# Sliding-window attention and two feed-forward layers on one core: weights rescaled seven block products behind their loads, x loaded a phase ahead

## The chip, the cores and the metric

One NeuronCore of a Trainium2 chip runs the whole program. The metric is the device time of one execution in microseconds; the median of several runs is compared. All times below are microseconds unless they say ns.

## The reference

```python
# attention: B=4, H=8, S=576, D=64, window 128, a slope per head
scores = scale * np.matmul(q, k.transpose(0, 1, 3, 2))
scores = np.where(mask, scores + bias[None], -1000000000.0)   # 0 <= i - j < 128
attn = softmax(scores)                                        # rows
x = np.matmul(attn, v) -> (2304 tokens, 512)
# layer 1: ELU                     # layer 2: SiLU
h = x @ w_in       # 512 -> 2048   h = x @ w_in
g = where(h > 0, h, exp(min(h,0)) - 1)   g = h * (1 / (1 + exp(-h)))
x = g @ w_out      # 2048 -> 512   out = g @ w_out
```

The weights arrive as 64-bit floats, q, k, v as 32-bit floats. The answer is wanted at 32-bit accuracy.

## The kernel before, in words

**Arithmetic.** Every 32-bit operand of a matmul is cut into an upper part (`...h`, a rounded copy made by ScalarE) and a lower part (`...l`, the difference, made by VectorE or GpSimd); a product is three matmuls, h·h, h·l and l·h. The products with `w_in` use a Strassen-like scheme: for a pair of two weight blocks and a block of 768 tokens, seven block products (`m1`, `m2`, `m6`, `m5`, `m7`, `m4`, `m3`, six matmuls each) take the place of eight.

**Phases.** `attention()` runs first and fills TensorE's idle time with the first four of 16 blocks of layer 1 (`hidden`, `output`). Then `layers()` runs: what is left of that filling (called the opening here), and then 15 steps `k`, written `(layer, sweep, token block)`. A sweep is a range of the 16 weight blocks (`SWEEPS`), and the three token blocks of 768 pass one after another. Step 0 to 2 and 3 to 5 are sweeps 1 and 2 of layer 1, steps 6 to 8, 9 to 11 and 12 to 14 are the sweeps of layer 2. A step is `nq` quads of seven block products, and then `outputs(k)`: 24 pieces (layer 1) or 18 (layer 2) of six matmuls each. The first quad of the next step takes the last two pieces along (`pend`), and each quad's `m4` and `m3` are made in the next quad or among the output pieces (`left_over`).

**Order.** The order on every engine is that in which the Python code issues instructions (`manual_schedule`), and every engine works through its own list in order: an instruction that waits holds all behind it on that engine. After each block product and each output piece `between(where)` is called. It moves each chain of activations one stage on (`chain`: `bent` exp or sigmoid on ScalarE, `act` on VectorE, `upper` the `gh` on ScalarE, `lower` the `gl` on GpSimd or VectorE), takes tasks from `xtasks`, and makes one step of the weights.

**Weights.** 128 x 512 blocks of 64-bit numbers are loaded into four raw tiles (`wraw`, `NRAW`), in the order of `tasks`. Each passes through four stages: `rescale` (GpSimd on the high words, line 144, and ScalarE on the low words, line 146), `sign` and `join` (VectorE, lines 151 and 156), and `part`, which makes the upper and lower parts. For `w_in` the second block of a pair first gets four sums on GpSimd (lines 186 to 189), and then `wbh`, `wch`, `wdh` on ScalarE with their lower parts on VectorE. Only then are the pair's two raw tiles free, and the loads that were issued into them on SyncE's queue can start. `weight_step(loaded, which, lag)` may take each stage once in a call; `rescale` follows its load by at least `lag` calls, and `part` waits for room in `made`/`room`. `room` for a new pair opens when the last step of a sweep has used the old one, so the weights of the next sweep are made during steps 2, 5, 8 and 11.

**x.** `make(k)` gives the tasks that make the seven operands of a new token block (`NAMES`, single buffered). Its two halves `c` are the even and the odd 128-row chunks of x. For layer 1 `begin(c)` loads the half from DRAM into `xs` (one buffer); for layer 2 it is taken from the accumulator. GpSimd makes four sums (lines 689 to 692), ScalarE the upper and VectorE the lower parts. Token blocks that come again are kept in DRAM (`keep`) and read back (`reload`).

```python
                calls[0] += 1
                weight_step(0, ((4, 1), (2, 3))[calls[0] % 2], 1)      # after an output piece
            elif where == "h":                                        # after a block product:
                calls[0] += 1                                         # every second time
                turn[0] += 1
                if turn[0] % 2 == 0:
                    weight_step(0, ((4, 1), (2, 3))[turn[0] // 2 % 2], 1)
```

Of the kernel before, what the change touches and what calls it, by code (L numbers as in the profile page):

```python
# [17 lines left out]
P = 128  # L18
# [24 lines left out]
def attention_elu_silu_kernel(  # L43
# [41 lines left out]
    OUTS = 7  # L85
    OPEN = 5
    ORDER = ((0, 1, 2), (2, 1, 0)), ((2, 1, 0), (0, 1, 2), (2, 1, 0))
    WSLOTS = [*range(15), *range(26, 34)]
# [556 lines left out]
    def layers(fill):  # L645
        pair_p.append(left("pair", PAIRS))
        c_p = left("combo", 1)
        h_p = left("hh", 2)
        e_p = left("ee", 3)
        t_p = left("tt", 1)  # L650
# [13 lines left out]
        NAMES = "b11", "b21", "b22", "t4", "t1", "t2", "t3"  # L664
        FIRST_USE = 0, 1, 5, 4, 6, 3, 2

# [5 lines left out]
        def make(k):  # L672

            layer, sw, b = steps[k]
            out = []
            src = {}

            def begin(c):
                if layer == 0:
                    src[c] = t = t_p.tile([P, 2, BIG], F32, tag="xs", name="xs")  # L680
                    nc.sync.dma_start(t, x_dram[b][:, c::2, :])
                else:
                    src[c] = acc[b].rearrange("p (c t) -> p c t", c=NKC)[:, c::2, :]

            def sums(c):
                b11, b12, b21, b22 = (src[c][:, i, j * HALF:(j + 1) * HALF] for i in range(2) for j in range(2))
                t2, t3, t4 = (t_p.tile([P, HALF], F32, tag=t, name=t) for t in ("t2", "t3", "t4"))
# [19 lines left out]
            def all_sums(c):  # L707
                for fn in sums(c):
                    fn()
            order = FIRST_USE  # L710
# [47 lines left out]
        def quad(k, q, last):  # L758
# [56 lines left out]
            def m4():  # L815
                product(3, "b", False)
                activated(t["b"][:, 0:HALF], 1, 0)
                if b == steps_last(k):
                    room[0] += 2

            def m3():
                product(2, "c", False)
                add("s2", "c")
                activated(t["s2"], 0, 1)
            return m1, m2, m6, m5, m7, m4, m3

# [55 lines left out]

        turn = [0]

        def between(where):
            chain()
            if where == "y":
                for _ in range(2):
                    if xtasks:
                        xtasks.pop(0)()  # L890
                calls[0] += 1
                weight_step(0, ((4, 1), (2, 3))[calls[0] % 2], 1)
            elif where == "h":
                calls[0] += 1
                turn[0] += 1
                if turn[0] % 2 == 0:
                    weight_step(0, ((4, 1), (2, 3))[turn[0] // 2 % 2], 1)

        for fn in make(0):
            xtasks.append(fn)  # L900
        seq = list(fill)
# [22 lines left out]
        while xtasks:  # L924
            xtasks.pop(0)()
        early.close()
# [5 lines left out]
        for k, (layer, sw, b) in enumerate(steps):  # L932
            nq = (SWEEPS[layer][sw][1] - SWEEPS[layer][sw][0]) // 2
            left_over = None
            for q in range(nq):
                for key in ((0, layer, SWEEPS[layer][sw][0] + 2 * q + 1),):
# [24 lines left out]
            while xtasks:  # L961
                xtasks.pop(0)()
        while chains:
# [36 lines left out]
```

## Time and profile before

| | |
|---|---|
| median of 3 runs | 1083.8 (1083.4 to 1087.84) |
| the profiled execution | 1088.96, of it span 1086.8 |
| TensorE matmul busy | 913.9 of the span (84%), mean granted clock 0.911 |
| VectorE busy | 631.8 (58%) |
| ScalarE busy | 490.6 (45%) |
| GpSimd busy | 423.6 (39%) |

How to read it: attention ends near 200, the opening near 252, and the 15 steps fill the rest. The granted clock is a share of full speed; in the trace it stands at one of two levels, 2.4 GHz and 1.2 GHz, and 128 x 384 matmuls of layer 1 begin 0.17 apart at the one level and 0.32 at the other. An engine's idle time counts only where TensorE ends up waiting for it.

### The profile page before, as it was taken

What the parts mean: (1) busy time and instruction counts of PE and PEld (TensorE: products, weight loads), DVE (VectorE), ACT (ScalarE), POOL (GpSimd) and SP (SyncE); (2) the same over time, 40 slices, a digit from 0 to 9 for tenths busy, and PEclk for the clock granted to TensorE, in tenths of its full rate; (3) what the DMA queues carried; (4) which work ended last, traced back from release to release, by engine and by line L of the source; (5) the groups of instructions that cost most, each with busy time, mean ns of one, the idle gap of its engine ahead of it and who ended that gap; (6) DMA issues with size and microseconds to landing.
All of it is one profiled execution on the core that took longest, in us unless ns stands there. A gap on an engine that the chain in (4) does not pass through costs nothing.

```text
span 1086.8 us, 15260 instructions
## 1 busy us (share of the span) xinstructions
PE 913.9 (84%) x5520; PEld 807.0 (74%) x5520; DVE 631.8 (58%) x1241; ACT 490.6 (45%) x1155; POOL 423.6 (39%) x514
## 2 busy tenths in 40 slices
PE   6789999954577997497999629989988899979998
PEld 4566767733577996397999629879876789968987
DVE  7866567345566766646464665767464643555444
ACT  6676667333542535334142444555544423344322
POOL 8643333146354435626141653625253411241111
PEclk9889999976778998798999869989988999989999
DMA  8324442211734211217050125251322605022551
GB/s 286 98 85 126 145 143 93 69 39 68 280 106 173 89 30 40 78 39 262 19 204 1 39 77 232 88 203 48 157 78 77 243 40 204 1 77 92 209 224 58
DMA packets 54923, 125.50 MB, mean 115 GB/s; under 512 B 3648, under 2 KB 35648, under 8 KB 54848
## 3 DMA queue, kind: packets, MB, share of 16 engines
q1 hardware_dynamic: 54704, 124.40, 32.0%
q8 instruction: 43, 0.70, 0.3%
q14 instruction: 32, 0.26, 0.1%
q10 hardware_dynamic: 144, 0.13, 0.0%
HBM read 87.56 MB, written 36.96 MB: 115 GB/s over the span
## 4 chain that ended last, share of the span: by engine, by line
PE 50%; DVE 14%; POOL 12%; issue 8%; ACT 8%; DMA 8%; SPq 0%; POOLq 0%; ACTq 0%; DVEq 0%
PE y L862 22%; PE b L775 10%; PE c L775 4%; DMA wraw<-in_moe_w_out_dram 4%; PE a L525 3%; POOL gl L755 3%; PE h L272 3%; DVE e L255 2%; PE a L775 2%; DMA wraw<-in_moe_w_in_dram 2%; DVE e L256 2%; PE y L308 2%; DVE wraw L151 2%; PE s L447 2%; PE pt L486 2%
## 5 line engine op out<-in xcount | busy, mean ns | idle before, releaser
L755 POOL TENSOR_TENSOR gl<-e,gh 128x384 fp32r<-128x384 f32 x120 | 128.9, 1079 | 303.7 <-ACT gh L751 242.9
L862 PE MATMUL y<-gh,w1h 128*128 128x384 f32 x288 | 102.8, 357 | 38.0 <-ACT gh L751 38.0
L751 ACT ACTIVATE gh<-e 128x384 fp32r<-128x384 f32 x168 | 86.4, 522 | 98.8 <-DVE e L256 60.7
L862 PE MATMUL y<-w1h,gl 128*128 128x512 f32 (+1 forms) x292 | 116.2, 398 | 5.4 <-DVE gl L755 5.4
L862 PE MATMUL y<-w1h,gh 128*128 128x512 f32 (+1 forms) x292 | 116.0, 397 | 5.0 <-ACT gh L751 5.0
L862 PE MATMUL y<-w1l,gh 128*128 128x512 f32 (+1 forms) x292 | 115.4, 395 | 0.0
L862 PE MATMUL y<-gl,w1h 128*128 128x384 f32 x288 | 103.6, 360 | 13.0 <-POOL gl L755 13.0
L151 DVE SCALAR_TENSOR_TENSOR wraw<-wraw 128x512 uint32<-128x512 uint32 x60 | 64.7, 1079 | 80.6 <-POOL wraw L144 80.6
L862 PE MATMUL y<-gh,w1l 128*128 128x384 f32 x288 | 101.5, 353 | 0.0
L506 POOL TENSOR_SCALAR p<-p,sm 128x192 f32<-128x192 f32 (+1 forms) x144 | 61.3, 444 | 101.4 <-DVE sm L464 91.4
L875 DVE TENSOR_TENSOR acc<-y,acc 128x384 f32<-128x384 f32 (+2 forms) x85 | 50.3, 605 | 74.4 <-PE y L862 74.4
L255 DVE TENSOR_SCALAR e<-e 128x384 f32<-128x384 f32 (+2 forms) x92 | 53.4, 580 | 64.3 <-ACT e L748 34.8
L862 PEld LDWEIGHTS y<-gh,w1h 128*128 128x128 f32 x288 | 58.1, 202 | 40.9 <-ACT gh L751 40.9
L146 ACT ACTIVATE wraw<-wraw 128x512 int32<-128x512 uint32 x60 | 40.2, 670 | 98.4 <-DMA wraw<-in_moe_w_out_dram 61.0
L460 ACT ACTIVATE p<-p,neg 128x192 f32<-128x192 f32 (+1 forms) x144 | 62.9, 439 | 31.7 <-DVE neg L455 31.7
L144 POOL TENSOR_SCALAR wraw<-wraw 128x512 f32<-128x512 f32 x60 | 41.3, 688 | 91.6 <-DMA wraw<-in_moe_w_out_dram 59.2
L166 POOL TENSOR_TENSOR w1l<-wraw,w1h 128x512 fp32r<-128x512 f32 x28 | 39.4, 1405 | 85.8 <-ACT w1h L165 85.8
L862 PEld LDWEIGHTS y<-w1h,gl 128*128 128x128 f32 x292 | 56.5, 193 | 19.4 <-DVE gl L755 7.1
L862 PEld LDWEIGHTS y<-gl,w1h 128*128 128x128 f32 x288 | 58.1, 202 | 16.8 <-POOL gl L755 16.7
L775 PE MATMUL b<-t,wdh 128*128 128x384 f32 x168 | 46.8, 361 | 25.9 <-ACT h L782 25.9
L862 PEld LDWEIGHTS y<-w1h,gh 128*128 128x128 f32 x292 | 56.8, 194 | 15.7 <-ACT gh L751 5.9
L782 ACT ACTIVATE hs<-b 128x384 f32<-128x384 f32 x42 | 20.4, 487 | 104.4 <-PE b L775 104.4
(146 smaller groups left out, 2391.0 us busy)
## 6 DMA issues: line engine op xcount, KB each, us to landing
t<-d SPq DMA_DIRECT2D x24, 768.0 KB, 6.7
wraw<-in_moe_w_in_dram SPq DMA_DIRECT2D x32, 512.0 KB, 4.1
d<-t SPq DMA_DIRECT2D x20, 768.0 KB, 6.2
wraw<-in_moe_w_out_dram SPq DMA_DIRECT2D x28, 512.0 KB, 3.6
b<-d SPq DMA_DIRECT2D x18, 768.0 KB, 5.6
d<-b SPq DMA_DIRECT2D x15, 768.0 KB, 4.5
k<-in_k_dram SPq DMA_DIRECT2D x16, 384.0 KB, 5.0
v<-in_v_dram SPq DMA_DIRECT2D x18, 256.0 KB, 2.8
```

The source lines that it names most:

```text
L144: nc.gpsimd.tensor_scalar(f32(top), f32(top), 2.0 ** -112, 1.0, op0=ALU.mult, op1=ALU.mult)
L146: nc.scalar.activation(low.bitcast(I32), low, AF.Copy, scale=7.49 * 2.0 ** -32)
L151: nc.vector.scalar_tensor_tensor(low, top, 0x80000000, low, op0=ALU.bitwise_and, op1=ALU.bitwise_or)
L166: eng.tensor_tensor(lo[:, o:o + w], f32(src), f32(h[:, o:o + w]), op=ALU.subtract)
L255: nc.vector.tensor_scalar(e, e, 1.0, -1.0, op0=ALU.min, op1=ALU.add)
L460: nc.scalar.activation(dst, dst, AF.Exp, bias=m, scale=-1.0, accum_out=a)
L506: nc.gpsimd.tensor_scalar(dst, dst, by, 1.0, op0=ALU.mult, op1=ALU.mult)
L751: nc.scalar.activation(gh[:, s], tiles["e"], AF.Copy)
L755: eng.tensor_tensor(gl[:, s], tiles["e"], f32(gh[:, s]), op=ALU.subtract)
L775: nc.tensor.matmul(t[name][:, 0:HALF], a[:, cs], x[:, j, c, :], start=(start and c == 0 and n == 0), stop=(c == 1 and n == 2), skip_group_ ...
L862: nc.tensor.matmul(t["ps"][:, 0:w], l, r, start=(f == 0 and x == 0), stop=(f == n - 1 and x == 2))
L875: nc.vector.tensor_tensor(dst, t["ps"][:, 0:w], dst, op=ALU.add)
```

## The change

**The lag.** Every `between` now makes one step of the weights, after block products too, and `rescale` follows its load by seven calls (`LAG`) and not by one. **x.** `make(k + 1)` is called at the start of step `k`, and `begin(0)` with it, so the load of the first half is issued some 21 block products before its sums; in layer 1 the sums then stand behind 21 empty tasks, and the second half's load and sums have 21 more between them. Three tasks are taken per output piece (`POPS`) and not two. The operands are made in the order b21, b11, t2, t1, t3, t4, b22, about the order in which the products of the step before let go of their places; the fourth sum is made later and in the place of `b21`, not in a tile of its own. **e.** The pool of activation tiles has four buffers and not three. **Room** for a new pair opens after `m3` and not after `m4`.

```diff
@@ class constants
+    LAG = 7
+    POPS = 3
@@ layers
-        e_p = left("ee", 3)
+        e_p = left("ee", 4)
@@ make
             def sums(c):
                 b11, b12, b21, b22 = (...)
-                t2, t3, t4 = (...)
-                src[c] = b11, b21, b22, t4, b12, t2, t3
-                return [lambda: nc.gpsimd.tensor_tensor(t3, b22, b12, op=ALU.subtract),
-                        lambda: nc.gpsimd.tensor_tensor(b12, b12, b11, op=ALU.subtract),
-                        lambda: nc.gpsimd.tensor_tensor(t2, b22, b12, op=ALU.subtract),
-                        lambda: nc.gpsimd.tensor_tensor(t4, b21, t2, op=ALU.subtract)]
+                t2, t3 = (...)
+                src[c] = b11, b21, b22, b21, b12, t2, t3
+                nc.gpsimd.tensor_tensor(t3, b22, b12, op=ALU.subtract)
+                nc.gpsimd.tensor_tensor(b12, b12, b11, op=ALU.subtract)
+                nc.gpsimd.tensor_tensor(t2, b22, b12, op=ALU.subtract)
+
+            def last_sum(c):
+                nc.gpsimd.tensor_tensor(src[c][1], src[c][1], src[c][5], op=ALU.subtract)
...
-            for c in range(2):
-                out.append(lambda c=c: (begin(c), all_sums(c)))
-                for x, i in enumerate((0, 1, 2, 6, 4, 5, 3)):
-                    out.append(lambda c=c, i=i: upper(c, i))
-                    if x:
-                        out.append(lambda c=c, i=last: lower(c, i))
-                    last = i
-                out.append(lambda c=c, i=last: lower(c, i))
+            def spread(c):
+                out = [lambda: sums(c)]
+                order = 1, 0, 5, 4, 6, 3, 2
+                for x, i in enumerate(order):
+                    out.append(lambda i=i: upper(c, i))
+                    if x:
+                        out.append(lambda i=order[x - 1]: lower(c, i))
+                    if x == 2:
+                        out.append(lambda: last_sum(c))
+                out.append(lambda: lower(c, order[-1]))
+                return out
+            begin_first = lambda: begin(0)
+            wait = [None] * (POPS * LAG if layer == 0 else 0)
+            out = spread(0) + [lambda: begin(1)] + wait + spread(1)
             if again(k):
                 out += [lambda i=i: keep(i) for i in range(7)]
-            return out
+            return begin_first, wait + out
@@ m4, m3: "room[0] += 2" moves from m4 to m3
@@ between
             if where == "y":
-                for _ in range(2):
+                for _ in range(POPS):
                     if xtasks:
-                        xtasks.pop(0)()
-                calls[0] += 1
-                weight_step(0, ((4, 1), (2, 3))[calls[0] % 2], 1)
-            elif where == "h":
-                calls[0] += 1
-                turn[0] += 1
-                if turn[0] % 2 == 0:
-                    weight_step(0, ((4, 1), (2, 3))[turn[0] // 2 % 2], 1)
+                        fn = xtasks.pop(0)
+                        fn and fn()
+            calls[0] += 1
+            weight_step(0, ((4, 1), (2, 3))[calls[0] % 2], LAG)
@@ the steps
+            if k + 1 < len(steps) and source(k + 1) == "make":
+                begin, ahead = make(k + 1)
+                begin()
             for q in range(nq):
...
             if k + 1 < len(steps) and source(k + 1) == "make":
-                xtasks.extend(make(k + 1))
+                xtasks.extend(ahead)
```

TensorE's own order is the same in both. **ScalarE in step 2**, around the first pair of the next sweep, before (`hs<-b` is the snap of a quad's first product, `wbh`, `wch`, `wdh` the upper parts of the pair, `wraw<-wraw` the rescaling of a block that has just been loaded, `h_...<-b` the snap of `m6`, for which `m7` waits):

```order
L782 ACTIVATE hs<-b 128x384
L751 ACTIVATE gh<-e 128x384
L748 ACTIVATE e<-hs 128x384
L165 ACTIVATE wbh<-wraw 128x256
L165 ACTIVATE wch<-wraw 128x512
L165 ACTIVATE wdh<-wraw 128x512
L146 ACTIVATE wraw<-wraw 128x512
L748 ACTIVATE e<-b 128x384
L782 ACTIVATE h_4386<-b 128x384
```

The same place in the changed kernel:

```order
L786 ACTIVATE hs<-b 128x384
L167 ACTIVATE wbh<-wraw 128x256
L167 ACTIVATE wch<-wraw 128x512
L167 ACTIVATE wdh<-wraw 128x512
L755 ACTIVATE gh<-e 128x384
L752 ACTIVATE e<-hs 128x384
L752 ACTIVATE e<-b 128x384
L786 ACTIVATE h_4378<-b 128x384
```

The rescaling has left the place ahead of the snap (it now stands behind the next pair's `wdh`), and the pair's upper parts stand one product earlier.

**GpSimd at the start of the opening**, before (`t<-xs` and `xs<-xs` are the sums of x for step 0, `wal` and `gl` lower parts, lines 186 to 189 a pair's sums, line 144 the rescaling):

```order
L689 TENSOR_TENSOR t_2893<-xs 128x384
L690 TENSOR_TENSOR xs<-xs 128x384
L691 TENSOR_TENSOR t_2892<-xs 128x384
L692 TENSOR_TENSOR t_2894<-xs,t_2892 128x384
L166 TENSOR_TENSOR wal<-wraw,wah 128x512
L291 TENSOR_TENSOR gl<-e,gh 128x512 x2
L186 TENSOR_TENSOR wraw<-wraw 128x256
L187 TENSOR_TENSOR wraw<-wraw 128x256
L188 TENSOR_TENSOR wraw<-wraw 128x256
L189 TENSOR_TENSOR wraw<-wraw 128x256
L144 TENSOR_SCALAR wraw<-wraw 128x512
```

and in the changed kernel:

```order
L168 TENSOR_TENSOR wal<-wraw,wah 128x512
L293 TENSOR_TENSOR gl<-e,gh 128x512 x2
L188 TENSOR_TENSOR wraw<-wraw 128x256
L189 TENSOR_TENSOR wraw<-wraw 128x256
L190 TENSOR_TENSOR wraw<-wraw 128x256
L191 TENSOR_TENSOR wraw<-wraw 128x256
L168 TENSOR_TENSOR wal<-wraw,wah 128x512
```

The four sums of x and the first rescaling have moved behind two pairs of weights.

**ScalarE at the end of the opening**, before (`b<-xs`, `t<-xs`, `t<-t` are upper parts of x's second half, `acc<-y` evictions):

```order
L697 ACTIVATE b_2899<-xs 128x384
L697 ACTIVATE b_2928<-xs 128x384
L165 ACTIVATE wah<-wraw 128x512
L146 ACTIVATE wraw<-wraw 128x512
L697 ACTIVATE b_2952<-xs 128x384
L697 ACTIVATE t_2996<-t_3066 128x384
L165 ACTIVATE wbh<-wraw 128x256
L165 ACTIVATE wch<-wraw 128x512
L165 ACTIVATE wdh<-wraw 128x512
L146 ACTIVATE wraw<-wraw 128x512
L697 ACTIVATE t_3013<-xs 128x384
```

and in the changed kernel:

```order
L148 ACTIVATE wraw<-wraw 128x512
L318 ACTIVATE acc_80<-y 128x512
L699 ACTIVATE b_3030<-xs 128x384
L699 ACTIVATE b_3032<-xs 128x384
L699 ACTIVATE t_3038<-t_3138 128x384
L699 ACTIVATE t_3047<-xs 128x384
L699 ACTIVATE t_3056<-t_3139 128x384
L699 ACTIVATE t_3059<-xs 128x384
L699 ACTIVATE b_3073<-xs 128x384
L786 ACTIVATE hs<-b 128x384
```

The seven upper parts now follow each other, with no weights among them, and the first snap of step 0 comes right behind.

## Rows read from the trace of the kernel before

**Rows 1.** Windows: stretch; length, busy (count) of PE, PEld, DVE, ACT, POOL; clock; DMA.

```profile
252.20:350.75 98.55, 60.25 (x260) 55.42 (x259) 60.29 (x86) 38.30 (x78) 46.68 (x45) 0.74 0.44 163
350.75:398.30 47.55, 47.24 (x271) 46.85 (x271) 33.31 (x52) 22.23 (x47) 21.69 (x20) 1.00 0.26 89
398.30:473.80 75.50, 52.71 (x272) 50.44 (x271) 46.78 (x68) 27.16 (x53) 35.03 (x35) 0.84 0.14 49
473.80:534.80 61.00, 52.58 (x272) 50.81 (x271) 34.45 (x51) 21.45 (x43) 24.16 (x22) 0.92 0.36 134
...
582.55:665.80 83.25, 53.80 (x271) 51.53 (x270) 48.94 (x69) 32.77 (x67) 43.51 (x43) 0.79 0.17 63
665.80:720.85 55.05, 50.08 (x235) 43.94 (x235) 42.70 (x62) 30.67 (x63) 26.13 (x24) 0.94 0.43 158
720.85:767.20 46.35, 46.35 (x235) 42.13 (x234) 27.58 (x41) 25.38 (x53) 15.88 (x14) 1.00 0.37 150
767.20:830.80 63.60, 52.27 (x235) 45.05 (x234) 35.50 (x48) 27.12 (x55) 28.97 (x29) 0.89 0.24 90
830.80:883.70 52.90, 48.64 (x236) 43.28 (x235) 29.47 (x44) 23.58 (x50) 16.50 (x17) 0.97 0.42 154
...
930.10:987.60 57.50, 48.95 (x235) 43.71 (x234) 32.38 (x47) 22.60 (x46) 20.86 (x21) 0.94 0.10 37
...
sum 887.80, PE 742.44 PEld 679.57 DVE 498.20 ACT 356.75 POOL 331.65; mean PE 49.50 PEld 45.30 DVE 33.21 ACT 23.78 POOL 22.11
```

**Rows 2.** TensorE's waits after 199: line <- releaser: total, times, longest.

```profile
PE y L862 <- ACT gh L751: 43.0, 9, 9.6
PE b L775 <- ACT h L782: 25.9, 5, 8.5
```

**Rows 3.** ScalarE's waits after 199, columns as before.

```profile
ACT wraw L146 <- DMA wraw<-in_moe_w_out_dram: 61.0, 16, 9.8
...
ACT wch L165 <- POOL wraw L188: 42.3, 13, 8.5
ACT wraw L146 <- DMA wraw<-in_moe_w_in_dram: 37.2, 10, 5.7
...
ACT e L748 <- POOL gl L755: 1.1, 1, 1.1
```

**Rows 4.** Timeline of ScalarE in step 2: start, length, instruction [idle before <-releaser].

```profile
419.49 0.67 ACT L165 ACTIVATE wch<-wraw 128x512 fp32r<-128x512 f32 x1 [0.96 <-POOL wraw L188]
...
424.82 0.66 ACT L146 ACTIVATE wraw<-wraw 128x512 int32<-128x512 uint32 x1 [3.97 <-DMA wraw<-in_moe_w_in_dram]
...
425.75 0.50 ACT L782 ACTIVATE h<-b 128x384 f32<-128x384 f32 x1
```

**Rows 5.** Timeline of SyncE's queue and of TensorE in step 2.

```profile
420.95 1.04 SPq L131 DMA_DIRECT2D wraw<-in_moe_w_in_dram  x2
426.29 1.01 PE L775 MATMUL b<-t,wdh 128*128 128x384 f32 x2 [6.91 <-ACT h L782]
```

**Rows 6.** Timelines of GpSimd and TensorE, opening and step 0.

```profile
217.86 1.02 POOL L689 TENSOR_TENSOR t<-xs 128x384 f32<-128x384 f32 x1 [18.70 <-issue]
280.74 1.01 PE L775 MATMUL b<-t,wch 128*128 128x384 f32 x2 [10.21 <-ACT hs L782]
```

**Rows 7.** Chain of work: start, length: the load of x's second half.

```profile
252.78 6.84 DMA xs<-xd
```

**Rows 8.** DMA, 180 to 345 in 40 slices: rate.

```profile
GB/s 0 6 64 2 4 0 0 132 317 2 0 0 0 254 0 0 0 94 328 22 0 0 188 382 402 413 335 81 46 113 14 127 2 249 196 6 0 0 191 167
```

**Rows 9.** Timeline of ScalarE in step 5.

```profile
627.87 0.67 ACT L165 ACTIVATE wch<-wraw 128x512 fp32r<-128x512 f32 x1 [8.54 <-POOL wraw L188]
```

**Rows 10.** Timeline of VectorE: the sign stage twice.

```profile
444.08 1.47 DVE L151 SCALAR_TENSOR_TENSOR wraw<-wraw 128x512 uint32<-128x512 uint32 x1 [3.67 <-POOL wraw L144]
463.24 0.69 DVE L151 SCALAR_TENSOR_TENSOR wraw<-wraw 128x512 uint32<-128x512 uint32 x1 [1.81 <-POOL wraw L144]
```

More of the change, by code (lines that the diff above doesn't have):

```diff
@@ L664, in layers @@
         NAMES = "b11", "b21", "b22", "t4", "t1", "t2", "t3"
-        FIRST_USE = 0, 1, 5, 4, 6, 3, 2
         def operand(k, i):
@@ L674, in make @@
             layer, sw, b = steps[k]
-            out = []
             src = {}
@@ L686, in sums @@
                 b11, b12, b21, b22 = (src[c][:, i, j * HALF:(j + 1) * HALF] for i in range(2) for j in range(2))
-                t2, t3, t4 = (t_p.tile([P, HALF], F32, tag=t, name=t) for t in ("t2", "t3", "t4"))
-                src[c] = b11, b21, b22, t4, b12, t2, t3
-                return [lambda: nc.gpsimd.tensor_tensor(t3, b22, b12, op=ALU.subtract),
-                        lambda: nc.gpsimd.tensor_tensor(b12, b12, b11, op=ALU.subtract),
-                        lambda: nc.gpsimd.tensor_tensor(t2, b22, b12, op=ALU.subtract),
-                        lambda: nc.gpsimd.tensor_tensor(t4, b21, t2, op=ALU.subtract)]
+                t2, t3 = (t_p.tile([P, HALF], F32, tag=t, name=t) for t in ("t2", "t3"))
+                src[c] = b11, b21, b22, b21, b12, t2, t3
[4 more added lines that the diff above has]
+                nc.gpsimd.tensor_tensor(src[c][1], src[c][1], src[c][5], op=ALU.subtract)
             def upper(c, i):
@@ L705, in keep @@
                 nc.sync.dma_start(d, f32(combos[k, i].rearrange("p x c t -> p (x c t)")))
[L707 to L710, printed above, removed]
-            for c in range(2):
-                out.append(lambda c=c: (begin(c), all_sums(c)))
-                for x, i in enumerate((0, 1, 2, 6, 4, 5, 3)):
-                    out.append(lambda c=c, i=i: upper(c, i))
-                    if x:
-                        out.append(lambda c=c, i=last: lower(c, i))
-                    last = i
-                out.append(lambda c=c, i=last: lower(c, i))
+            def spread(c):
[3 more added lines that the diff above has]
+                    out.append(lambda i=i: upper(c, i))
+                    if x:
+                        out.append(lambda i=order[x - 1]: lower(c, i))
[6 more added lines that the diff above has]
+            out = spread(0) + [lambda: begin(1)] + wait + spread(1)
             if again(k):
                 out += [lambda i=i: keep(i) for i in range(7)]
-            return out
+            return begin_first, wait + out
         def reload(k, i):
@@ L817, in m4 @@
                 activated(t["b"][:, 0:HALF], 1, 0)
-                if b == steps_last(k):
-                    room[0] += 2
             def m3():
@@ L824, in m3 @@
                 activated(t["s2"], 0, 1)
+                if b == steps_last(k):
+                    room[0] += 2
             return m1, m2, m6, m5, m7, m4, m3
@@ L881, in outputs @@
             return ([p for g in first for p in g[:-1]] + [g[-1] for g in first] + [p for g in rest for p in g])
-        turn = [0]
         def between(where):
@@ L887, in between @@
             if where == "y":
-                for _ in range(2):
+                for _ in range(POPS):
                     if xtasks:
-                        xtasks.pop(0)()
-                calls[0] += 1
-                weight_step(0, ((4, 1), (2, 3))[calls[0] % 2], 1)
-            elif where == "h":
-                calls[0] += 1
-                turn[0] += 1
-                if turn[0] % 2 == 0:
-                    weight_step(0, ((4, 1), (2, 3))[turn[0] // 2 % 2], 1)
-        for fn in make(0):
-            xtasks.append(fn)
+                        fn = xtasks.pop(0)
+                        fn and fn()
+            calls[0] += 1
+            weight_step(0, ((4, 1), (2, 3))[calls[0] % 2], LAG)
+        begin, xs0 = make(0)
+        begin()
+        xtasks.extend(xs0)
         seq = list(fill)
@@ L924, in layers @@
         while xtasks:
-            xtasks.pop(0)()
+            fn = xtasks.pop(0)
+            fn and fn()
         early.close()
@@ L934, in layers @@
             left_over = None
+            if k + 1 < len(steps) and source(k + 1) == "make":
+                begin, ahead = make(k + 1)
+                begin()
             for q in range(nq):
@@ L961, in layers @@
             while xtasks:
-                xtasks.pop(0)()
+                fn = xtasks.pop(0)
+                fn and fn()
         while chains:
```

## The prediction

> **What bounds the kernel now.** I read the windows first, one for each step, because the steps hold equal work. Step 1 takes 47.55, TensorE busy 47.24 at full clock, and step 7 46.35: there TensorE alone sets the time [rows 1]. The other steps of the same size take longer, at a lower clock. What a step takes above these two is its excess. Step 0 (98.55; it lacks two carried pieces, and a piece or product is 47.55 / 45 = 1.06, so 45.4 would do) has 53.1; step 2 27.95, step 5 35.7; step 8 17.25, step 11 11.15; steps 3, 6 and 9 13.45, 8.7 and 6.55. Together 173.9 [rows 1]. These are the opening and the steps in or after which a sweep's weights are made.
>
> Then TensorE's waits: the longest are for ScalarE, 43.0 for `gh` among the output pieces and 25.9 for the snap `h` [rows 2]. ScalarE's own waits say why: 61.0 + 37.2 = 98.2 in 26 waits of line 146 for a load that has just been issued, and 42.3 of `wch` for GpSimd's pair sums [rows 3]. The timeline of step 2 shows one such wait whole: the loads start at 420.95, ScalarE stands at the rescaling until 424.82, the snap behind it is made at 425.75, and TensorE starts `m7` at 426.29 after 6.91 idle [rows 4, 5].
>
> **The change part by part.**
>
> *Lag, step 2.* The pair's sums on GpSimd are where they were, so `wch` stays at about 419.5 and `wdh` ends at about 420.9 [rows 4]. Then come one `gh`, two exp and the snap, each about 0.5, the first exp behind a VectorE add that waits for `wdl`: the snap ends at about 423.6 where it now ends at 426.25. 4.2 of the 6.91 stay. The two longer waits for `gh` later in this step (the list's longest is 9.6 [rows 2]) were ScalarE standing at line 146 as well. The rescaling of the next load now stands behind the second pair's `wdh`, by my count at about 432, some 7 after its data has landed (420.95 + 3.9), so it waits for nothing. What I see left is 4.2, some 2 of half clock behind it, and 2.3 for late `gl`: 8.5 of 27.95, a gain of 19.5. Bounds: nothing, and all 27.95.
>
> *Lag, step 5.* Here x for step 6 is summed on GpSimd ahead of the second pair's sums, in both orders: the wait of 8.54 for them [rows 9] shrinks little, and the last `gl` stands behind the second half's sums and the third pair's. I count a first stall of 3.5, then some 15 among the last output pieces, and 6 of half clock: 25 of 35.7 stay, a gain of 11 (bounds 0 and 30).
>
> *Lag, steps 8 and 11.* The same pattern as step 2 without x. With the same share left (8.5 / 27.95 = 0.30) 12.0 and 7.8 are gained, 20 together. *Steps 3, 6 and 9* wait for what the loads of the last two raw fills still hold up; I did not follow them wait by wait and take half of 28.7, 14 (bounds 0 and 28.7).
>
> *x, opening and step 0.* GpSimd now stands 18.70 at the first sum [rows 6], and pairs and `gl` behind it; in the changed order two pairs go first. That brings the end of the opening forward, but TensorE then waits for x's second half: its load stands in SyncE's queue behind that of raw block 12, which waits until the pair of blocks 8 and 9 is split. Their rescaling has moved back, so I leave the load at 252.8, landing 259.6 [rows 7] (5 earlier or later are possible). Now weights follow between the upper parts; afterwards there are none: three sums of about 1.1 [rows 6], the rest of the upper parts at 0.5, and the first snap, after which `m6` can start, at 265.5 where it is now 280.74 [rows 6]. From there TensorE needs 45.4 less two products, 43.3; now it takes 350.75 - 280.74 = 70.0 [rows 1, 6]. New there: all seven stores of `keep` are issued together, then x for step 1, then raw block 14. Six transfers of 768 KB at 383 GB/s, the mean of the slices 382, 402, 413 and 335 [rows 8], are 12.3, so block 14 lands at about 279 while ScalarE comes to its rescaling at about 273: 6 of ScalarE, 3.5 of TensorE and 2 of half clock. With 3 of half clock at the start and 3 for GpSimd's `gl`, the rest is 54.8 and step 0 ends at 320.3, a gain of 30 (bounds: 0, and the excess of 53.1).
>
> *Steps 0 to 2, x a phase ahead.* Steps 1 and 7 have no excess [rows 1], so the earlier load and the order b21, b11, t2 gain nothing there; the 21 empty tasks leave the last upper parts about four pieces (4.2) before the next step, about what three sums take (3.3). I price this at 0, up to 3 a step lost. Hidden by the output pieces.
>
> *Fourth e tile.* ScalarE waited 1.1 in all for a `gl` to free one [rows 3]: 0, at most 1. *Room at m3, fewer GpSimd tiles*: one product later, 0.
>
> *More at once.* My replay used durations as they stand; VectorE's sign stage takes 0.69 or 1.47 [rows 10], and I take the long form to be the one beside GpSimd work. With less waiting more of it overlaps: 0.8 for some ten joins on the path, 8 lost.
>
> The sum: 30 + 19.5 + 11 + 20 + 14 - 8 = 86.5. The profiled execution took 1088.96, so 1002.5; it lies 5.2 above the median of 1083.8, which gives **997**.
>
> **The rivals.**
>
> *VectorE and GpSimd take turns.* If the two never worked at once, the 887.8 after 199 could not shrink below 498.20 + 331.65 = 829.9 [rows 1]: 199 + 829.9 + 2.2 - 5.2 = 1026. For it: the sign stage that is twice as long [rows 10]. Against it: the short form exists, and many VectorE instructions read PSUM. The Trainium skill (SBUF — State Buffer, section "SBUF: two separate sides") says that VectorE with two SBUF inputs and GpSimd lock a shared port pair, one of them blocked for the whole instruction of the other; by that rule held for every instruction the time is this rival's, and rows 10 agree with it in direction only.
>
> *The wait moves to the pair sums.* ScalarE no longer waits for loads and so comes sooner to `wch`, where it waits for GpSimd (42.3 [rows 3]). If each of the 14 pairs' `wch` waits grows by the mean 98.2 / 26 = 3.8 that it no longer spends at line 146, 53 is given back: 1083.8 - (94.5 - 53) = 1042. For it: 8.54 in step 5 [rows 9]. Against it: in step 2 `wch` came ahead of the rescaling and waited only 0.96 [rows 4].
>
> *The lag is used up.* The loads start some 9 after their place in the order (420.95 [rows 5], the first of them issued at about 412), and seven products are 7.4: if ScalarE came to the rescaling on time it would still wait to 424.8, and x's load is no earlier: no change, 1084. Against it: ScalarE has the second pair ahead of the rescaling.
>
> *The weights come too late* (slower). A sweep fills the four raw tiles three times (the last twice), 14 fills; each is longer by 7.4. If TensorE had to wait for every one, 104 is lost against 86.5 gained: 1101. It decides where a fill outlasts the work that covers it: the next sweep's first pairs lie ready in raw tiles, and the rest is due only 45 products and pieces later (47.55 [rows 1]). Against it: the order has the last `w1h` of a sweep well before the output pieces that use it.
>
> **How the numbers follow.** Chances: forecast 0.58 (its own range 972 to 1020, from the load of x 5 off, step 5 and steps 3, 6, 9 between half and double what I left), take turns 0.14, pair sums 0.17, used up 0.04, too late 0.07. The range from **965 to 1045** holds the first three, and reaches below for terms that keep less than I left. Half a per cent, 5.4, is about what a measurement of this kernel can tell from no change. Faster 0.90, from the first three; same 0.03, slower 0.07.
>
> **What would show it.** In the profile after: ScalarE's waits at the rescaling fall from 98.2 to under 25, most of what is left in step 0 behind the stores; step 2 near 56, step 5 near 72, steps 8 and 11 near 52 and 50; step 1 and 7 unchanged; `m6` of step 0 starts near 265. I am wrong if `wch` waits grow past 80 (pair sums), if step 1 or 7 gets longer (x too late), if TensorE waits for `w1h` or a pair at the start of a step (weights too late), or if step 0's `m6` stays at 280.

## The result and the profile after

The changed kernel takes 1026.35 (median of 4 runs, 1024.96 to 1027.41), the kernel before 1085.57 beside it (1083.4 to 1087.84): a ratio of 0.945 with a 95% interval of 0.943 to 0.948, faster by 5.5%. The forecast was 997 and its range 965 to 1045. The span falls by 61.2, from 1086.8 to 1025.6, where the sum had 86.5.

Of the 61.2, 2.7 lie in attention, whose code is the same in both. Timeline of SyncE's queue, attention's last store of x, before and after:

```profile
210.37 0.53 SPq L250 DMA_DIRECT2D xd<-x  x1
```

```profile
207.63 0.53 SPq L252 DMA_DIRECT2D xd<-x  x1
```

In the traces of all kernels below this store stands between 204.9 and 210.8, so where the end of the opening matters I count from it.

Windows of the changed kernel, columns as in [rows 1], for steps 0, 2, 3, 5, 6, 8, 9 and 11:

```profile
240.40:331.70 91.30, 54.45 (x259) 50.24 (x258) 64.43 (x89) 38.81 (x80) 48.27 (x47) 0.79 0.39 139
...
379.90:440.70 60.80, 52.47 (x271) 50.39 (x271) 44.25 (x67) 29.56 (x58) 37.06 (x38) 0.92 0.18 61
440.70:500.00 59.30, 52.17 (x272) 50.12 (x272) 37.57 (x56) 21.35 (x43) 24.88 (x22) 0.91 0.38 138
...
547.70:621.05 73.35, 53.48 (x271) 51.93 (x271) 51.42 (x73) 33.03 (x67) 42.57 (x43) 0.81 0.22 79
621.05:675.20 54.15, 48.83 (x235) 43.13 (x235) 42.95 (x58) 30.95 (x63) 28.78 (x24) 0.97 0.42 157
...
721.60:774.00 52.40, 49.43 (x236) 44.33 (x235) 30.87 (x44) 26.99 (x55) 26.30 (x27) 0.93 0.29 106
774.00:828.40 54.40, 50.53 (x236) 44.26 (x235) 31.69 (x48) 24.00 (x49) 19.41 (x19) 0.94 0.44 159
...
874.80:925.20 50.40, 48.21 (x235) 43.64 (x234) 32.41 (x47) 22.49 (x46) 21.15 (x21) 0.97 0.12 42
```

Beside [rows 1], the steps that make weights are shorter: step 2 by 14.7, step 5 by 9.9, step 8 by 11.2, step 11 by 7.1, and step 0 ends 19.0 earlier (16.3 counted from attention's last store). Steps 3, 6 and 9 together lose only 1.1.

Waits of the changed kernel after 197, columns as in [rows 2] (line numbers are two to four higher than before: the rescaling on ScalarE is line 148):

```profile
ACT wch L167 <- POOL wraw L190: 52.7, 14, 7.2
...
ACT wraw L148 <- DMA wraw<-in_moe_w_out_dram: 16.8, 8, 5.6
PE b L779 <- DVE hs L789: 15.7, 9, 7.5
PE b L779 <- ACT h L786: 12.7, 7, 3.7
PE y L866 <- ACT gh L755: 11.2, 6, 5.4
```

ScalarE's 98.2 at the rescaling [rows 3] has become 16.8. TensorE's 43.0 for `gh` and 25.9 for `h` [rows 2] have become 11.2 and 12.7. `wch` has grown from 42.3 only to 52.7.

Three places remain in the opening and step 0. Timeline of SyncE's queue, ScalarE, VectorE and TensorE:

```profile
253.63 0.56 SPq L681 DMA_DIRECT2D xs<-xd  x1
262.34 0.69 PE L779 MATMUL b<-b,wah 128*128 128x384 f32 x1 [20.10 <-ACT b L699]
267.57 0.62 PE L779 MATMUL b<-t,wch 128*128 128x384 f32 x2 [0.51 <-ACT hs L786]
268.71 4.01 SPq L707 DMA_DIRECT2D d<-t  x4
274.13 2.61 SPq L137 DMA_DIRECT2D wraw<-in_moe_w_out_dram  x2
285.22 0.66 ACT L148 ACTIVATE wraw<-wraw 128x512 int32<-128x512 uint32 x1 [5.60 <-DMA wraw<-in_moe_w_out_dram]
285.97 1.47 DVE L153 SCALAR_TENSOR_TENSOR wraw<-wraw 128x512 uint32<-128x512 uint32 x1 [4.66 <-POOL wraw L146]
289.61 0.55 DVE L789 TENSOR_TENSOR hs<-b,hs 128x384 f32<-128x384 f32 x1
290.21 1.01 PE L779 MATMUL b<-t,wbh 128*128 128x384 f32 x2 [7.53 <-DVE hs L789]
```

TensorE waits 20.10 for the parts of x's second half, whose load is issued at 253.63; `m6` then starts at 267.57. Raw block 14 is issued at 274.13, behind the seven stores and x's next load. ScalarE stands 5.60 for it; VectorE's sign and join then stand ahead of the add that `m4` waits for, and TensorE stands 7.53.

### The profile page after: what moved, and what is told of

Read it like the earlier page. It is cut to its first block, busy times and chain, and to the rows that moved or that the text cites. A ratio compares the mean times of both kernels' runs of the same rounds, so it can differ in the third digit from the quotient of the medians.

```text
span 1025.6 us, 15310 instructions
## 1 busy us (share of the span) xinstructions
PE 900.2 (88%) x5520; PEld 798.6 (78%) x5520; DVE 633.1 (62%) x1241; ACT 490.6 (48%) x1155; POOL 427.2 (42%) x514
## 4 chain that ended last, share of the span: by engine, by line
PE 51%; DVE 15%; POOL 13%; ACT 9%; issue 7%; DMA 4%; POOLq 0%; DVEq 0%; SPq 0%; ACTq 0%
PE y L866 24%; PE b L779 9%; PE c L779 5%; DVE e L257 3%; PE a L527 3%; DVE e L258 3%; PE h L274 3%; PE y L310 2%; POOL gl L759 2%; PE a L779 2%; DVE wraw L153 2%; DMA wraw<-in_moe_w_out_dram 2%; PE s L449 2%; PE pt L488 2%; ACT e L752 2%
## 5 line engine op out<-in xcount | busy, mean ns | idle before, releaser
L759 POOL TENSOR_TENSOR gl<-e,gh 128x384 fp32r<-128x384 f32 x120 | 131.1, 1095 | 321.6 <-ACT gh L755 297.0
L866 PE MATMUL y<-gl,w1h 128*128 128x384 f32 x288 | 100.9, 350 | 15.2 <-POOL gl L759 15.2
L866 PE MATMUL y<-gh,w1h 128*128 128x384 f32 x288 | 100.3, 348 | 9.8 <-ACT gh L755 9.8
L508 POOL TENSOR_SCALAR p<-p,sm 128x192 f32<-128x192 f32 (+1 forms) x144 | 61.5, 445 | 100.7 <-DVE sm L466 90.8
L879 DVE TENSOR_TENSOR acc<-y,acc 128x384 f32<-128x384 f32 (+2 forms) x85 | 50.3, 605 | 81.1 <-PE y L866 81.1
L257 DVE TENSOR_SCALAR e<-e 128x384 f32<-128x384 f32 (+2 forms) x92 | 51.9, 565 | 52.7 <-ACT e L752 30.9
L153 DVE SCALAR_TENSOR_TENSOR wraw<-wraw 128x512 uint32<-128x512 uint32 x60 | 57.9, 965 | 26.2 <-POOL wraw L146 24.9
L866 PEld LDWEIGHTS y<-w1h,gl 128*128 128x128 f32 x292 | 56.0, 192 | 15.2 <-DVE gl L759 3.8
L752 ACT ACTIVATE e<-hs 128x384 f32<-128x384 f32 x84 | 44.1, 525 | 47.3 <-DVE hs L789 47.0
L866 PEld LDWEIGHTS y<-gh,w1h 128*128 128x128 f32 x288 | 57.0, 198 | 11.1 <-ACT gh L755 11.1
L168 POOL TENSOR_TENSOR w1l<-wraw,w1h 128x512 fp32r<-128x512 f32 x28 | 40.1, 1431 | 59.5 <-ACT w1h L167 42.9
L866 PEld LDWEIGHTS y<-w1l,gh 128*128 128x128 f32 x292 | 55.9, 191 | 9.6
L779 PE MATMUL b<-b,wah 128*128 128x384 f32 x168 | 44.0, 340 | 22.1 <-ACT b L699 20.1
```

The lines of the kernel that those rows point to most:

```text
L153: nc.vector.scalar_tensor_tensor(low, top, 0x80000000, low, op0=ALU.bitwise_and, op1=ALU.bitwise_or)
L168: eng.tensor_tensor(lo[:, o:o + w], f32(src), f32(h[:, o:o + w]), op=ALU.subtract)
L257: nc.vector.tensor_scalar(e, e, 1.0, -1.0, op0=ALU.min, op1=ALU.add)
L508: nc.gpsimd.tensor_scalar(dst, dst, by, 1.0, op0=ALU.mult, op1=ALU.mult)
L752: nc.scalar.activation(e, src, AF.Exp if layer == 0 else AF.Sigmoid)
L759: eng.tensor_tensor(gl[:, s], tiles["e"], f32(gh[:, s]), op=ALU.subtract)
```

## The experiments

My theory was that the loss lay in ScalarE and GpSimd standing at the rescaling of a block whose load had just been issued. The rivals were that x's new order frees the engines, or that the more frequent weight step does it; for steps 3, 6 and 9, VectorE's sign and join among the products stood against work that merely arrives late.

Length of each step (from the starts of its first block product on TensorE's timeline to that of the next; "open" is all ahead of step 0), the median, and the ratio to the kernel before with its interval:

| kernel | open | 0 | 1 | 2 | 3 | 5 | 6 | 8 | 9 | 11 | median | ratio |
|---|---|---|---|---|---|---|---|---|---|---|---|---|
| before | 252.2 | 98.6 | 47.6 | 75.5 | 61.0 | 83.3 | 55.0 | 63.6 | 52.8 | 57.6 | 1085.57 | 1 |
| changed | 240.4 | 91.3 | 48.2 | 60.8 | 59.3 | 73.3 | 54.2 | 52.4 | 54.4 | 50.4 | 1026.35 | 0.945 (0.943 to 0.948) |
| e1 lag only | 246.4 | 90.6 | 47.6 | 62.2 | 58.9 | 72.5 | 54.7 | 55.5 | 52.8 | 57.7 | 1040.98 | 0.957 (0.953 to 0.960) |
| e2 x only | 250.8 | 96.0 | 51.4 | 70.3 | 64.9 | 81.5 | 61.2 | 56.6 | 65.6 | 53.8 | 1091.39 | 1.004 (1.002 to 1.006) |
| e3 lag 3 | 240.8 | 97.9 | 47.6 | 70.6 | 61.4 | 78.6 | 54.2 | 56.2 | 62.6 | 54.6 | 1068.42 | 0.982 (0.979 to 0.985) |
| e4 every 2nd | 241.3 | 84.2 | 54.7 | 59.8 | 56.1 | 69.4 | 54.6 | 50.7 | 53.6 | 47.8 | 1014.41 | 0.932 (0.929 to 0.936) |
| e5 late stores | 241.6 | 84.6 | 48.8 | 59.7 | 59.2 | 73.3 | 54.2 | 49.7 | 57.1 | 50.3 | 1021.01 | 0.939 (0.935 to 0.942) |
| e6 x first | 243.1 | 89.1 | 49.5 | 60.9 | 59.5 | 73.5 | 54.5 | 49.7 | 57.1 | 50.3 | 1026.89 | 0.945 (0.942 to 0.947) |
| e7 quarter join | 237.0 | 87.2 | 47.6 | 57.9 | 58.0 | 71.6 | 49.5 | 51.2 | 49.3 | 50.4 | 1000.27 | 0.920 (0.917 to 0.923) |
| e9 room at m4 | 242.0 | 88.4 | 49.0 | 63.8 | 60.2 | 74.8 | 53.8 | 55.5 | 52.9 | 57.7 | 1039.80 | 0.957 (0.954 to 0.960) |
| e10 lag, room | 246.2 | 90.8 | 47.6 | 58.2 | 59.0 | 69.8 | 57.1 | 50.9 | 54.2 | 49.0 | 1026.30 | 0.944 (0.941 to 0.947) |
| e11 room later | 241.6 | 88.3 | 49.1 | 61.8 | 61.8 | 70.5 | 54.7 | 52.4 | 55.4 | 50.0 | 1026.76 | 0.944 (0.942 to 0.946) |
| e12 combination | 243.5 | 93.2 | 49.2 | 59.9 | 56.4 | 69.4 | 54.3 | 50.6 | 52.4 | 47.7 | 1016.29 | 0.934 (0.932 to 0.936) |
| e13 lag, room, every 2nd | 245.9 | 93.4 | 47.6 | 58.6 | 55.6 | 68.9 | 53.4 | 50.6 | 52.7 | 47.7 | 1021.20 | 0.940 (0.937 to 0.942) |

The changed kernel, e5 and e6 run the same instructions in the same order from step 2 on, and still differ by up to 2.7 in a step. So I read nothing from a difference under 3 in a single step. "Open" holds attention too, and so its scatter of up to 5.9.

**e1, the weights' part alone**, on the kernel before:

```diff
-                calls[0] += 1
-                weight_step(0, ((4, 1), (2, 3))[calls[0] % 2], 1)
-            elif where == "h":
-                ...
+            calls[0] += 1
+            weight_step(0, ((4, 1), (2, 3))[calls[0] % 2], LAG)
```

> The weights' part alone: a weight step behind every piece and product, the rescaling seven calls behind its load; x, its sums, the e tiles and the room as before. If ScalarE and GpSimd standing at the rescaling was the loss (my theory), steps 2, 5, 8 and 11 shrink as they did with the whole change, by 14.7 + 9.9 + 11.2 + 7.1 = 42.9: about 1043, at most 6 away, and the end of the opening stays. If the gain hangs on x and its sums, which free GpSimd (the rival), it stays above 1070.

1040.98, the time expected, but not its parts: steps 2, 5 and 8 shrink by 13.3, 10.8 and 8.1 and step 11 not at all, while the end of the opening, which was to stay, comes 5.8 earlier, and step 0 is 8.0 shorter. **e2, the rest alone**, the changed kernel with the old `between` of the weights:

> The rest of the change alone: x loaded a phase ahead, three tasks a piece, sums in the new order, four e tiles, room at the last product; the weight steps come as before, the rescaling one call behind its load. My theory: only the part ahead of step 1 shrinks, by 19 or somewhat less, about 1066, and steps 2, 5, 8, 11 keep their length. The rival (x frees the engines): below 1050.

1091.39: both expectations missed. Even the opening gains little, and what steps 2, 5, 8 and 11 lose (5.2, 1.8, 7.0 and 3.8) comes back in steps 1, 3, 6 and 9 (3.8, 3.9, 6.2 and 12.8). ScalarE's waits at the rescaling, first e1's, then e2's two rows:

```profile
ACT wraw L147 <- DMA wraw<-in_moe_w_out_dram: 11.1, 5, 3.2
```

```profile
ACT wraw L148 <- DMA wraw<-in_moe_w_out_dram: 58.4, 20, 6.9
ACT wraw L148 <- DMA wraw<-in_moe_w_in_dram: 39.0, 10, 5.4
```

With the lag the waits go, without it all 97.4 stay and nothing is gained.

**e3, a shorter lag**: `weight_step(..., 3)` in place of `LAG`.

> The changed kernel with a lag of three calls in place of seven. Three calls are about 3.2, and ScalarE's mean wait for a load in the kernel before was 3.8 behind one. If the lag in time is what counts, some load waits of 1 to 3 each return, 1032 to 1045. If it is the weight step at every call that counts and not the lag (the rival), it stays within 5 of 1026.

1068.42: the lag counts, the weight step at every call does not by itself. The kernel before had a lag of one already, so three calls add two, some 2.1, to it; of the mean wait of 3.8 some 1.7 should be left, and 46.1 in 22 waits (2.1 each) is. Those waits are as expected, but they cost 42 and not the 6 to 19 that I allowed:

```profile
ACT wraw L148 <- DMA wraw<-in_moe_w_out_dram: 40.4, 19, 9.1
ACT wraw L148 <- DMA wraw<-in_moe_w_in_dram: 5.7, 3, 2.0
```

**e9, the room as before**: the two lines `if b == steps_last(k): room[0] += 2` go back from `m3` to `m4`.

> The changed kernel with the room for the next sweep given at the last but one product as before. I priced this at 0: 1023 to 1029. The rival: one call earlier turns the order of the two kinds of weight step against the products, so that the halves of a pair stand ahead of a snap; then steps 8 and 11 go back to the 55.5 and 57.7 that the kernel with the weights' part alone has: about 1036.

1039.80: an edit that I priced at 0 is worth 13, 10.4 of it in steps 8 and 11, which the rival named. TensorE's waits for VectorE's adds, 15.7 in the changed kernel (above), are in e9:

```profile
PE b L779 <- DVE hs L789: 43.2, 17, 7.4
```

Timeline of e9 in step 11, VectorE and TensorE:

```profile
907.79 1.33 DVE L153 SCALAR_TENSOR_TENSOR wraw<-wraw 128x512 uint32<-128x512 uint32 x1 [1.83 <-POOL wraw L146]
...
910.28 0.96 DVE L759 TENSOR_TENSOR gl<-e,gh 128x384 fp32r<-128x384 f32 x1
911.30 0.50 PE L866 MATMUL y<-w1h,gl 128*128 128x512 f32 x1 [2.38 <-DVE gl L759]
...
914.03 0.54 DVE L789 TENSOR_TENSOR hs<-b,hs 128x384 f32<-128x384 f32 x1
914.63 0.69 PE L779 MATMUL b<-t,wbh 128*128 128x384 f32 x1 [2.83 <-DVE hs L789]
```

and the same place in the changed kernel, with TensorE's only wait of that step:

```profile
895.47 1.00 PE L779 MATMUL b<-t,wch 128*128 128x384 f32 x2 [2.19 <-ACT hs L786]
...
901.60 0.56 DVE L789 TENSOR_TENSOR hs<-b,hs 128x384 f32<-128x384 f32 x1 [0.22 <-ACT wah L167]
903.64 1.50 DVE L153 SCALAR_TENSOR_TENSOR wraw<-wraw 128x512 uint32<-128x512 uint32 x1 [1.48 <-POOL wraw L146]
```

In e9 a `gl` stands behind sign and join, and an `hs` add behind the pair's lower parts (the last, `wdl`, at 913.43); TensorE waits 2.38 and 2.83. With room a little later the add is made at 901.60, ahead of the sign stage, and TensorE's only wait in that step is one of 2.19.

**e10, lag and room alone**, e1 with the room of the changed kernel:

> The kernel before with two edits of the change alone: the weight step at every call with the lag of seven, and the room for the next sweep given at the last product. If lag and room are all of the change, the 13 between the rooms come on top of the lag's: 1026 to 1030, with x loaded and summed as before. If room helps only because x's work is out of GpSimd's way (the rival), it stays at 1036 to 1041.

1026.30, the time of the changed kernel: lag (with the weight step at every call) and room are all of the gain. **e11, the room one call later still**:

```diff
-                    room[0] += 2
+                    late["room"] = 2
...
             weight_step(0, ((4, 1), (2, 3))[calls[0] % 2], LAG)
+            room[0] += late.pop("room", 0)
```

> The changed kernel with the room given one call later still, behind the weight step that follows the last product. If what room did was to set the phase of the two kinds of weight step against the products, one more call turns it back: steps 8 and 11 go to about 55.5 and 57.7, and the kernel takes 1034 to 1042. If it is merely better to begin the next sweep's pairs later (the rival), it stays within 3 of 1026 or falls below.

1026.76, so steps 8 and 11 stay. My reading by phase rested on a wrong count: between `m4` and `m3` stands another product or an output piece, so their calls are two apart and the kind of weight step is the same at both. What the rows of e9 and of the changed kernel show is that the second pair's sign stage now begins behind the add of the step's last products; one turn more costs nothing.

**e5, the stores later**, `keeps` being filled by `make(0)` in place of the tasks:

```diff
+            if where == "h":
+                turn[0] += 1
+                if turn[0] > 5 and keeps:
+                    keeps.pop(0)()
```

> The changed kernel with the seven stores of step 0's combinations issued one behind each product from the sixth on, so that the loads of raw blocks 14 to 17 stand ahead of most of them in the queue. If the stores are what block 14 waits for, ScalarE's wait of 5.60 at its rescaling and TensorE's 7.53 behind it go, step 0 falls from 91.3 to about 83 and the kernel takes 1017 to 1020. The rival: something else is late at the same place, or the gain is given back at step 1, which waits for x's second half: 1024 to 1028.

1021.01, between the two ranges, 1.0 above the first; step 0 takes 84.6. The wait of 5.60 is gone; at its place (285.38) TensorE still waits 3.39 for VectorE's add, which stands behind a sign of 1.48 and a join of 1.36.

**e6, x's load ahead of block 12**: for `k == 0` the first run of empty tasks is two calls shorter, the second two calls longer.

> The changed kernel with the sums of x's first half two calls earlier in the opening, so that the load of the second half is issued ahead of that of raw block 12 and stands no longer behind it; the second half's tasks keep their place. If the order in the queue is what TensorE's wait of 20.10 ends with, GpSimd starts the second half's sums at about 257.5, right behind the rescaling of block 12 (256.84 and 0.64), instead of 261.40, and m6 is 4 earlier: about 1022. The rival: the opening ends with the weights of blocks 8 to 12, and no more than 1 is gained.

1026.89, no gain: the rival. Timeline of e6, SyncE's queue and GpSimd:

```profile
249.33 0.56 SPq L681 DMA_DIRECT2D xs<-xd  x1
261.04 0.64 POOL L146 TENSOR_SCALAR wraw<-wraw 128x512 f32<-128x512 f32 x1 [3.29 <-DVE wraw L158]
261.65 0.99 POOL L689 TENSOR_TENSOR t<-xs 128x384 f32<-128x384 f32 x1
```

The load is issued at 249.33 and not 253.63, but the sums are made at 261.65, behind the rescaling of block 12, which has itself moved from 256.84 to 261.04. Of that, 2.9 is attention's (its last store is at 210.53); for the rest, the first half's sums now stand ahead of a pair's sums on GpSimd. Counted from that store `m6` starts after 58.6, in e9 and e11, whose opening is that of the changed kernel, after 57.4 and 57.5 (in its own trace after 59.9). So nothing is gained, but the edit moved the weights too, and which of the two sets the end of the opening stays open.

**e4, the weight step at every second product**, the lag still seven calls:

```diff
+            if where == "y":
+                weight_step(0, ((4, 1), (2, 3))[calls[0] % 2], LAG)
+            else:
+                turn[0] += 1
+                if turn[0] % 2 == 0:
+                    weight_step(0, ((4, 1), (2, 3))[turn[0] // 2 % 2], LAG)
```

> The changed kernel with the weight step behind every second block product as before, the lag still seven calls. If the steps 3, 6 and 9 keep their excess because VectorE's sign and join come at every product and hold up its adds, these steps lose about half of their excess of 11.75, 8.1 and 8.0, and the kernel takes about 1013. If the spacing doesn't matter (the rival), it stays within 5 of 1026; if weights now end too late for the output pieces, it is above 1035.

1014.41, the time I expected, but not for the reason: steps 3, 6 and 9 lose only 3.6 together. Step 0 loses 7.1, and step 1 gives 6.5 of it back, since x's second half lands where it did, and TensorE waits 3.04 behind it:

```profile
328.18 0.94 ACT L699 ACTIVATE b<-xs 128x384 fp32r<-128x384 f32 x2 [7.92 <-DMA xs<-xd]
```

The 12 lie in steps 2, 3, 5, 8 and 11, at 1.0 to 3.9 each.

**e7, sign and join over a quarter of the columns** (`t[:, 0:NKC * P // 4, ...]` in both).

> The changed kernel with VectorE's sign and join stages over a quarter of the columns (the other three quarters of the weights are not joined), which takes about 58 of VectorE's 633. If VectorE's work among the products is what holds steps 3, 6 and 9 above 47.6 and 46.4, they fall by 20 together and the others follow: 985 or less. If VectorE is late only because what it works on is late (the rival), less than 10 is gained: above 1015.

1000.27, between the two. VectorE's busy time falls by 57.7, from 633.1 to 575.4. Windows of e7 for steps 3, 6 and 9:

```profile
429.66:487.68 58.02, 52.92 (x272) 51.07 (x271) 32.23 (x55) 21.38 (x43) 23.07 (x23) 0.91 0.40 141
606.97:656.49 49.52, 46.99 (x236) 41.92 (x236) 36.20 (x52) 30.67 (x63) 26.91 (x24) 1.00 0.44 165
754.09:803.35 49.26, 47.49 (x235) 41.96 (x234) 24.16 (x46) 23.29 (x48) 17.96 (x18) 1.00 0.48 169
```

Steps 6 and 9 lose 4.7 and 5.1 of some 8 and stay at full clock; step 3 keeps 10.4 of its 11.7.

**e12, a combination**: e4, e5, and no empty tasks ahead of the first half's sums in steps 1 and 2.

> The changed kernel with the weight step behind every second product, the seven stores of step 0 behind its products, and no empty tasks ahead of the first half's sums of x in steps 1 and 2. With the wider step alone 1014; step 1 took 54.7 there, where x's second half landed at 328 and TensorE had been ready since 325. If that load is all that is late, step 1 goes back to about 48 and the kernel takes 1005 to 1009. The rival: the sums, now earlier, hold up the gl of step 0's last output pieces on GpSimd, and nothing is gained: 1012 to 1017.

1016.29: the rival. Step 1 goes to 49.2, but step 0 to 93.2. GpSimd makes three sums (308.17 to 312.35) ahead of a `gl` of step 0's own output pieces, and ScalarE's parts of x stand among their `gh`:

```profile
321.26 0.45 PE L867 MATMUL y<-gh,w1h 128*128 128x384 f32 x1 [2.14 <-ACT gh L756]
```

Keeping x's work away from these pieces is what the empty tasks are for. **e13, the kernel before with the lag of seven and the room at `m3`** and nothing else (its weight step comes at every second product anyway):

> The kernel before with two edits alone: the rescaling seven calls behind its load, with the weight step still behind every second product, and the room given at the last product. If x's part and the weight step at every product are worth nothing here, it is as fast as the changed kernel or faster; with the steps of the wider spacing (84 in step 0, 47.6 in step 1 as with x's old order, 59.8, 56.1 and 69.4 in 2, 3 and 5, 50.7 and 47.8 in 8 and 11) behind an opening of 246: 1007 to 1012. The rival: with x's old order the wider spacing makes the weights or x late in step 0 and 1: 1014 to 1026.

1021.20, the rival: step 0 takes 93.4 where e4 with x's new order has 84.2. With the wider spacing x's part is worth 7 (0.932 against 0.940): it gains 9.2 in step 0 and loses 7.1 in step 1, and step 7, not in the table, takes 50.4 in e13 and 46.4 in all others, TensorE waiting 2.20 for a lower part of x at 674.42. e4 has the lowest median of the versions that leave nothing out.

## Why the prediction was right, and what was wrong in it

The direction and the main mechanism were right: with the lag ScalarE no longer stands at the rescaling (98.2 to 16.8, the forecast "under 25"), e1 gains 47.8 from it alone (1088.81 to 1040.98, of the changed kernel's 59.2), and e2 nothing without it. By the steps of the prediction:

- **Steps 3, 6 and 9, the step that failed.** "I did not follow them wait by wait and take half of 28.7": 14 was forecast, 1.1 came. The premise, that these steps wait for loads, already failed in the kernel before. Timeline of its step 3, VectorE and TensorE:

```profile
492.03 0.68 DVE L151 SCALAR_TENSOR_TENSOR wraw<-wraw 128x512 uint32<-128x512 uint32 x1
...
493.35 0.55 DVE L785 TENSOR_TENSOR hs<-b,hs 128x384 f32<-128x384 f32 x1
493.95 0.62 PE L775 MATMUL b<-t,wbh 128*128 128x384 f32 x2 [3.25 <-DVE hs L785]
```

  The add stands behind sign and join, and ScalarE's last rescaling ahead of it (488.31) had waited only 0.68 for a load. TensorE's one longer wait in that step, 3.79 at 506.83, is for a `gl` of GpSimd, and step 9's longest, 2.96 at 857.3, stands behind sign and join again. TensorE's waits in step 3 sum to 8.4 before and 7.1 after. Timeline of the changed kernel in step 3, VectorE, ScalarE and TensorE:

```profile
460.57 1.50 DVE L153 SCALAR_TENSOR_TENSOR wraw<-wraw 128x512 uint32<-128x512 uint32 x1
...
462.72 0.55 DVE L789 TENSOR_TENSOR hs<-a,hs 128x384 f32<-128x384 f32 x1
463.36 0.52 ACT L752 ACTIVATE e<-hs 128x384 f32<-128x384 f32 x1 [2.15 <-DVE hs L789]
...
465.81 1.01 PE L779 MATMUL b<-t,wdh 128*128 128x384 f32 x2 [2.86 <-ACT h L786]
```

  No load is waited for here either. The add stands behind sign and join, ScalarE's exp waits 2.15 for the add, and the snap, with an upper part and a rescaling still ahead of it, is made at 465.27. e7 shows that sign and join are part of it: 11.1 of the three steps' excess goes with three quarters of that work, 9.8 of it in steps 6 and 9. At this place in step 3 e7 still waits 2.07. What is left of step 3 there (10.4: 5.4 because TensorE's busy time is 52.92, at a granted clock of 0.91, where a step at full clock takes 47.5, the rest in waits) stays open.
- **End of the opening and step 0: 16.3 and not 30** (19.0 by the clock of the trace, 2.7 of it attention's). Counted from attention's last store `m6` starts 10.4 earlier (13 in e9 and e11, with the same opening), where 15.2 were forecast: that 267.57 lies so near 265.5 is in part luck. The rest took 64.1 (331.7 less 267.6) and not 54.8. ScalarE's wait for block 14 came as forecast (5.60 for 6), with both of its ends some 6 later; the sum counted six transfers of 768 KB ahead of the block, where seven stores and x's load are eight. What was undersized is the stall behind it, 7.53 on TensorE and not 3.5, for VectorE's sign and join stand between that wait and the add; step 0 loses 6.7 without the stores there (e5). I also put the earlier end of the opening down to x's order. From attention's last store step 0 starts after 41.8 before, 36.1 in e1 and e10, where x is as before, and 32.8 in the changed kernel: 5.7 of the 9.0 come with the weights.
- **Step 2: 14.7 and not 19.5; step 5: 9.9 for 11; steps 8 and 11: 18.3 for 20.** In step 2 the snap is waited for 3.66 (4.2 forecast); half clock is what was undersized: TensorE is busy 52.47 where 47.24 do at full clock [rows 1], 5.2 and not 2. In step 5 the terms hold: 3.58 at the first stall, 16.3 among the last output pieces, 6.2 of half clock. Step 11's size is luck: with the lag alone it stays at 57.7, and it is the room that shortens it. **Room at `m3`**, priced at 0, is worth 13 (e9). I had counted its product of delay and not what VectorE does for the pair in the meantime.
- **x a phase ahead: 0** in steps 1 and 7 was right. As a whole x's part is worth nothing here: the changed kernel and e10 take the same time. The end of step 1 lies 4.7 earlier (379.9 against 384.6), 2.5 of it attention's; the rest is within the scatter. The fourth e tile was never changed alone.
- **VectorE and GpSimd more at once: 8 lost** did not come. VectorE's sign stage over the whole execution, before and after (busy time, mean ns):

```profile
L151 DVE SCALAR_TENSOR_TENSOR wraw<-wraw 128x512 uint32<-128x512 uint32 x60 | 64.7, 1079 | 80.6 <-POOL wraw L144 80.6
```

```profile
L153 DVE SCALAR_TENSOR_TENSOR wraw<-wraw 128x512 uint32<-128x512 uint32 x60 | 57.9, 965 | 26.2 <-POOL wraw L146 24.9
```

  It got shorter, not longer. Without this term the sum is 94.5, and the span misses 33.3 of it: 11 in the opening and step 0 (13.7, less attention's 2.7), 4.8 in step 2, 12.9 in steps 3, 6, 9 and about 4.6 in small terms; the wrong 8 hid that much of it. The other 4 of the 29 in the median lie in the median of before, which is 1083.8 in the three runs I used and 1085.6 to 1088.8 in those beside the later runs.

The rivals: the wait did not move to the pair sums (52.7, far from the 42.3 + 53 it would need), the lag was not used up, and the weights were not late. **VectorE and GpSimd taking turns** gave 1026, the time that was measured, and yet not by its mechanism. Window of the changed kernel from 197 on:

```profile
197.00:1025.60 828.60, 730.64 (x3699) 672.52 (x3694) 499.32 (x745) 356.71 (x729) 335.57 (x323) 0.93 0.32 119
```

VectorE's 499.32 and GpSimd's 335.57 are 834.9 in 828.6: busy time includes the time that one is held by the other, so their sum is no bound. And if it set the time, e7 would gain all that sign and join got shorter. From step 2 on their busy time falls from 77.6 to 43.4, so by 34.2; that stretch falls by 17 (645.7 to 628.6). VectorE's 126 adds from PSUM last 0.54 to 0.56 throughout. The Trainium skill (SBUF — State Buffer, section "SBUF: two separate sides") says that a VectorE instruction with two SBUF inputs and a GpSimd one that reads SBUF exclude each other for the whole instruction; e7's rows below agree with that for sign and join (1.08 for 0.28).

## What to carry to other kernels

When an engine issues work on data whose load was just queued, put the use several calls behind the load, and size the lag by the waits in the trace, counting from the lag that is there: raised by two calls it left 46.1 of the 98.2 here, raised by six 16.8. An edit that moves only when a batch of work may begin is not free: count what the shared engines have in their queues ahead of the instruction that the bound engine waits for. Before taking a share of a step's excess as one kind of wait, follow that step's waits once.

## What the hardware showed that I had not expected

VectorE's sign and join, beside a GpSimd instruction, are held by a time that doesn't depend on their own size. Timeline of e7, where sign and join have a quarter of the columns, VectorE and GpSimd:

```profile
454.76 1.00 POOL L759 TENSOR_TENSOR gl<-e,gh 128x384 fp32r<-128x384 f32 x1
454.83 1.08 DVE L153 SCALAR_TENSOR_TENSOR wraw<-wraw 128x128 uint32<-128x128 uint32 x1 [1.80 <-POOL wraw L146]
...
458.62 0.28 DVE L153 SCALAR_TENSOR_TENSOR wraw<-wraw 128x128 uint32<-128x128 uint32 x1
```

Alone the quarter takes 0.28, beside a `gl` of 1.00 it takes 1.08; the whole stage takes 0.69 or 1.50 (above, and [rows 10]). Both are held by about 0.8, which is what was left of the `gl`, less 0.13 to 0.15. So it goes throughout: in 37 sign and join instructions of the changed kernel and 32 of e7 that began, after attention, with over 0.2 of a GpSimd instruction left, the time beyond 0.69 or 0.28 is what was left, less 0.12 to 0.17. So cutting such an instruction's size doesn't shorten the hold; moving it away from GpSimd's work would by these rows save it, which was not tried.
